# Cutting the first row maximum of each period into 128 and 384 columns, sharing the copy of the value products, and a new order of the period, in an attention and gated-MLP kernel

## The chip, the cores and the metric

The kernel runs on one core of one Trainium2 chip. The metric is the device time of one execution in microseconds (us); lower is better. The profile shown is of one execution, taken by the hardware profiler.

## The reference

```python
# x [1, 2048, 512]; H = 32 heads of Dh = 16
qkv = (x @ wqkv).reshape(B, S, 3, H, Dh).transpose(2, 0, 3, 1, 4)
scores = einsum("bhqd,bhkd->bhqk", q, k) * Dh ** -0.5
o = einsum("bhqk,bhkd->bhqd", softmax(scores), v)
a = o.transpose(0, 2, 1, 3).reshape(B, S, D) @ wo
b = (sigmoid(x @ w_gate) * (x @ w_up)) @ w_down          # F = 1792
g = sigmoid((x * gate_w).sum(-1, keepdims=True))
out = g * a + (1 - g) * b                                # all float32
```

## The kernel before

TensorE (PE) multiplies, ScalarE (ACT) does the exponentials and copies, VectorE (DVE) the row maxima and other copies, GpSimd (POOL) sums, SyncE (SP) issues transfers. Matrices stand as a high and a low part, so that a product of two of them takes three matmuls.

The kernel opens with the projections of the first heads and of the values. Then comes a loop over 256 periods (`for k in range(NPER)`), 16 for each pair of heads; a period deals with two 128-row blocks of keys and half of the queries. Its parts, by the words of the string `STEADY`:

- `m0`, `m1`: the row maxima of a later pair (11 periods ahead), four products of each of the two heads in a period. One takes a score product on PE (L294, 48 rows, 512 columns) into a PSUM tile, and VectorE reduces it to a column of `stat` (L296).
- `t0`, `t1`: four score products of each head (L684), each followed by an exponential on ACT that writes a quarter of a tile `p` (L686). `t1` works one period ahead.
- `d0`, `d1`: six matmuls each (L163) of the sums that fill the rest of PE: projections of later heads and the gate and up products. `d0` uses the lower 64 rows of the PE and `d1` the upper 64, as the two heads do: two products of 64 rows run side by side, one in each half. They write `dn`, which ACT copies out at the end of a period (L609). At `turn` PE waits for a token of POOL, since both halves write one bank.

After these words `values(k)` (L842 to L857) issues eight value products (L848), which the profile counts as 16 matmuls; each writes 17 of the 128 rows of one tile. ACT then copies that tile to `part` or `sum` (L853, 512 columns), and POOL adds `part` to `sum` (L865). From period 245 on (`k >= FREE`) there are no maxima left, another order (`LAST`) holds, and VectorE does that copy (L855). A last part multiplies by `w_down` and `wo`.

The instructions of PE, ACT, DVE and POOL stand in the order in which the code issues them. The layer below writes the semaphore waits. Eight PSUM tiles of one bank each: `dn`, `sm0` to `sm3` (numbers 0 to 3 in the order's words) and `st0` to `st2` (4 to 6). A word such as `m1:3` takes number 3; the value products of each period take number 0 (`SUMS`).

```python
STEADY = ("m1:3 t0:2 m0:4 d1 d1 t0:5 m0:6 d1 d1 t0:1 d1 m0:3 d1 t0:2 turn m0:0 t1:4 "
          "m1:5 d0 d0 t1:1 t1:6 d0 d0 m1:2 d0 m1:3 t1:4 d0")
...
spot[:] = [seven[SUMS]]
values(k)
```

Of the kernel before, what the change touches and what calls it, by code (L numbers as in the profile page):

```python
# [24 lines left out]
S, D, H, DH, F = 2048, 512, 32, 16, 1792  # L25
P = 128
# [20 lines left out]
def gated_mix(ctx, tc, x, xT, wqk, wv, wo, w_gate, w_up, w_down, gate_w, out):  # L47
    nc = tc.nc
    pe, act, dve, pool, sp = nc.tensor, nc.scalar, nc.vector, nc.gpsimd, nc.sync
# [6 lines left out]
    def turns(tiles):  # L56
        turn = iter(range(1 << 30))
        return lambda: tiles[next(turn) % len(tiles)]
# [124 lines left out]
    def work(length):  # L183
# [4 lines left out]
            length -= cost  # L188
        over[0] = max(0.0, -length)

    def flush(queue):
        while queue:
            queue.pop(0)[1]()
# [79 lines left out]
    stat = {}  # L273
# [7 lines left out]
    def sm_step(j):  # L281

        p, s = divmod(j, 32)
        qt, kh = divmod(s, 2)
        qs, ks = QS[p % 2], KS[p % 2]
        half = (p, qt // 8)
        if half not in stat:
            stat[half] = keep.tile([P, 2, 8, 4], F32, name=f"stat{p}_{qt // 8}", tag="stat", bufs=2)
            count[half] = 0

        def one(b, i):
            r, g = 64 * b, 2 * kh + i
            t = bankm()
            pe.matmul(t, qs[r:r + KM, qt * P:(qt + 1) * P], ks[r:r + KM, g * 512:(g + 1) * 512],  # L294
                      start=True, stop=True)
            dve.tensor_reduce(stat[half][:, b, qt % 8, g:g + 1], t, axis=AX.X, op=ALU.max)  # L296
            count[half] += 1
            if count[half] == 64:
                m = mpad()
                dve.tensor_reduce(m[:, :16].rearrange("p (a b) -> p a b", a=2), stat.pop(half), axis=AX.X, op=ALU.max)  # L300
                mt = mrow[half] = keep.tile([P, 32], F32, name=f"mt{p}_{qt // 8}", tag="mt", bufs=2)
                dve.transpose(mt, m)  # L302
        return one

    def put_max(half):
# [309 lines left out]
    def first_max():  # L615
        if first:
            j, i = first.pop(0)
            one = sm_step(j)
            one(0, i)
            one(1, i)  # L620

    for c in range(NC):
        if c + 1 < NC:
# [49 lines left out]
    def st_part(k, b):  # L673

        p, r = divmod(2 * k, 32)
        i, kt = divmod(r, 16)
        qs, ks = QS[p % 2], KS[p % 2]
        r = 64 * b
        pt = ptile[k, b] = mid(f"p{k}_{b}")
        for a in range(2):  # L680
            for c in range(2):
                o = bank()
                q0 = i * 1024 + c * 512
                pe.matmul(o, ks[r:r + KR, (kt + a) * P:(kt + a + 1) * P], qs[r:r + KR, q0:q0 + 512],  # L684
                          start=True, stop=True)
                act.activation(pt[:, 2 * a + c, :], o, AF.Exp, scale=DH ** -0.5)  # L686
                yield

    bank = turns(early)
    ahead = st_part(0, 1)  # L690
# [22 lines left out]
                put_v(t + a, two[a].o, dve if n == 14 or (n == 15 and a == 0) else act)  # L713


    seven = maxb + banks
    bank7 = turns([seven[b] for b in (5, 1, 6, 2, 3, 4, 0)])
    chunks = [(c, f) for c in range(NC) for f in range(0, NF, 2)]

    def hidden_load(c, f):  # L720
# [119 lines left out]
    def values(k):  # L840

        o = bank()  # L842
        half = divmod(k // 8, 2)
        pts = [ptile.pop((k, b)) for b in range(2)]
        for a in range(2):
            for c in reversed(range(4)):
                h = 2 * half[0] + c // 2
                pe.matmul(o[32 * c:32 * c + VW, :], v[:, 2 * k % 16 + a, h * VW:(h + 1) * VW],  # L848
                          pts[c // 2][:, 2 * a + c % 2, :], start=(a == 0), stop=(a == 1))

        def put(e):
            if 2 * k + LEAD < NSTEP:
                act.activation(e, o, AF.Copy)  # L853
            else:
                dve.tensor_copy(e, o)  # L855
        if half not in sums:
            sums[half] = keep.tile([P, 512], F32, name=f"sum{half[0]}_{half[1]}", tag="sum", bufs=2)  # L857
            put(sums[half])
        else:
            e = keep.tile([P, 512], F32, name=f"part{k}", tag="part", bufs=2)  # L860
            put(e)
            later.append((1.3, lambda s=sums[half]: add(s, e)))

        def add(s, e):
            pool.tensor_tensor(s, s, e, ALU.add)  # L865
            if k % 8 == 7:
                sp.dma_start(pv_d[half[1], half[0]], s)

    def mx(b):
        for j in range(LEAD, NSTEP):  # L870
            one = sm_step(j)
            for i in range(2):
                one(b, i)
                yield

    dens = [chain(denominators(0, 0, 32, 8), denominators(1, 0, 32, 8)), denominators(0, 32, 64, 2),
            denominators(1, 32, 64, 2)]
# [5 lines left out]
            yield  # L883

    spot = []

    def emit(order, **parts):

        for word in order.split():
            if word == "turn":  # L890
                if run:
                    turn(run)
                work(2.0)
            else:
                kind, _, b = word.partition(":")
                spot[:] = [seven[int(b)]] if b else []
# [4 lines left out]
    BEGIN = " ".join(w[:-1] + {"1": "5", "5": "1"}.get(w[-1], w[-1]) if ":" in w else w for w in STEADY.split())  # L901
# [4 lines left out]
    bank = bankm = lambda: spot[0]  # L906
    for k in range(NPER):
        n = 2 * k
        if n + LEAD == NSTEP:
            bank = bank7  # L910
            leave = dve.tensor_copy
        if 75 <= k < 123:
            t, r = divmod(k - 75, 6)
            if r in (0, 3):
                split_load(2 * t + r // 3)
            if r in (1, 4):
                split_sum(2 * t + r // 3)
            if r == 1:
                logit_load(2 * t)
            if r in (3, 4):  # L920
                logits(2 * t, r - 3)
        if n % 32 == 0 and n // 32 + 1 < NPAIR:
            load_pair(n // 32 + 1)
        parts["t0"], parts["t1"] = st_part(k, 0), st_part(k + 1, 1) if k + 1 < NPER else iter(())
        emit(BEGIN if k == 0 else STEADY if k < FREE else LAST, **parts)
# [35 lines left out]
    bank = turns(banks[:1])  # L961
    loaded.extend(hidden_load(*chunks[m]) for m in range(2, 4))
    raws.extend(late_raw(*late[m][:2]) for m in range(2, 4))
    loaded.extend(hidden_load(*chunks[m]) for m in range(4, 6))
# [28 lines left out]
        split(oh, ol, ot, act, pool)  # L993
        return oh, ol

    bankt = turns([dn, maxb[1], banks[2], maxb[2], maxb[3]])
    bankh = turns([maxb[0], banks[0], banks[1]])
    acc, had = {}, {}

    def finish(t, o, gate):  # L1000
# [28 lines left out]
    for n, (c, f) in enumerate(chunks):  # L1029
# [5 lines left out]
        for t in range(4):  # L1035
            ops = list(terms([((hl[0][:, a, t * P:(t + 1) * P], hl[1][:, a, t * P:(t + 1) * P]), wd[f + a])
                              for a in range(2)]))
            for m, (a, b) in enumerate(ops):
                pe.matmul(down[t], a, b, start=(f == 0 and m == 0), stop=(f == NF - 2 and m == 5))  # L1039
            if f == NF - 2:  # L1040
                finish(4 * c + t, down[t], g0)
            if (n, t) == (0, 1):
                values(NPER - 1)
                flush(later)
        if n < 3:
            next(dens[1], None)
# [47 lines left out]
```

## Time and profile before

| | |
|---|---|
| median of 3 runs | 1683.34 us (1683.09 to 1683.47) |
| the profiled execution | 1682.99 us, its span 1681.0 us |
| granted PE clock | 1.00 |
| PE busy | 1675.7 us (100%) |
| DVE busy | 1453.0 us (86%) |
| ACT busy | 1360.9 us (81%) |
| POOL busy | 942.5 us (56%) |

The 2.0 us beside the span are start and end of the execution. A busy time is the sum of an engine's own intervals. Matmuls overlap each other in a pipeline and their ends are modelled, so a PE that is always busy need not be one that can do no more.

### The profile page before, as it was taken

What the parts mean: (1) busy time and instruction counts of PE and PEld (TensorE: products, weight loads), DVE (VectorE), ACT (ScalarE), POOL (GpSimd) and SP (SyncE); (2) the same over time, 40 slices, a digit from 0 to 9 for tenths busy, and PEclk for the clock granted to TensorE, in tenths of its full rate; (3) what the DMA queues carried; (4) which work ended last, traced back from release to release, by engine and by line L of the source; (5) the groups of instructions that cost most, each with busy time, mean ns of one, the idle gap of its engine ahead of it and who ended that gap; (6) DMA issues with size and microseconds to landing.
All of it is one profiled execution on the core that took longest, in us unless ns stands there. A gap on an engine that the chain in (4) does not pass through costs nothing.

```text
span 1681.0 us, 34649 instructions
## 1 busy us (share of the span) xinstructions
PE 1675.7 (100%) x12485; PEld 1060.1 (63%) x12485; DVE 1453.0 (86%) x2350; ACT 1360.9 (81%) x2656; POOL 942.5 (56%) x922
## 2 busy tenths in 40 slices
PE   9999999999999999999999999999999999999999
PEld 7766656565656565656565665656565656568887
DVE  7988888888889999999888888889999888887753
ACT  4188888898988898889898989889898989983431
POOL 1134476547656666566666767676666667653110
PEclk9999999999999999999999999999999999999999
DMA  8411447366565564555535353434343434368862
GB/s 271 119 46 59 130 171 211 133 171 206 145 198 136 164 151 154 160 166 188 160 103 146 102 146 108 134 103 133 109 134 105 133 114 158 123 206 277 288 217 70
DMA packets 143788, 254.20 MB, mean 151 GB/s; under 512 B 24256, under 2 KB 36544, under 8 KB 140736
## 3 DMA queue, kind: packets, MB, share of 16 engines
q1 hardware_dynamic: 135024, 235.34, 46.3%
q10 hardware_dynamic: 8592, 16.65, 3.1%
q8 instruction: 98, 1.61, 0.4%
q14 instruction: 74, 0.61, 0.1%
HBM read 149.42 MB, written 102.50 MB: 150 GB/s over the span
## 4 chain that ended last, share of the span: by engine, by line
PE 99%; DVE 0%; DMA 0%; ACT 0%; ACTq 0%; issue 0%; DVEq 0%
PE dn L163 30%; PE sm L848 27%; PE sm L294 16%; PE sm L1039 5%; PE st L684 5%; PE sm L684 5%; PE st L294 2%; PE dn L1039 2%; PE st L1039 2%; PE st L163 2%; PE st L150 1%; PE st L646 1%; PE sm L150 1%; PE st L848 1%; DVE stat L296 0%; DMA x<-in_xT_dram 0%
## 5 line engine op out<-in xcount | busy, mean ns | idle before, releaser
L296 DVE TENSOR_REDUCE stat<-sm 128x1 f32<-128x512 f32 x1314 | 848.2, 681 | 136.6 <-PE sm L684 125.8
L686 ACT ACTIVATE p<-sm 128x512 f32<-128x512 f32 x1030 | 611.0, 630 | 11.3 <-PE st L163 10.1
L686 ACT ACTIVATE p<-st 128x512 f32<-128x512 f32 x1018 | 615.6, 651 | 0.0
L294 PE MATMUL sm<-ks,qs 48*128 48x512 f32 x1314 | 525.2, 435 | 0.0
L848 PE MATMUL sm<-p,v 128*17 128x512 f32 x4016 | 479.9, 595 | 0.0
L296 DVE TENSOR_REDUCE stat<-st 128x1 f32<-128x512 f32 x734 | 478.8, 680 | 0.0
L684 PE MATMUL sm<-qs,ks 64*128 64x512 f32 x1030 | 428.6, 419 | 0.0
L684 PE MATMUL st<-qs,ks 64*128 64x512 f32 x1018 | 425.5, 419 | 0.0
L294 PEld LDWEIGHTS sm<-ks,qs 48*128 48x128 f32 x1314 | 241.0, 184 | 261.7 <-DVE stat L296 214.9
L865 POOL TENSOR_TENSOR sum<-sum,part 128x512 f32<-128x512 f32 x224 | 288.6, 1288 | 135.5 <-PE sm L684 121.7
L294 PE MATMUL st<-ks,qs 48*128 48x512 f32 x734 | 290.0, 395 | 0.0
L848 PEld LDWEIGHTS sm<-p,v 128*17 128x17 f32 x4016 | 93.1, 96 | 224.3 <-issue 155.4
L853 ACT ACTIVATE part<-sm 128x512 f32<-128x512 f32 x214 | 128.3, 600 | 124.1 <-issue 84.1
L544 POOL TENSOR_TENSOR chain<-chain,chain 128x512 f32<-128x512 f32 x96 | 124.3, 1294 | 155.4 <-PE sm L684 140.4
L684 PEld LDWEIGHTS st<-qs,ks 64*128 64x128 f32 x1018 | 187.3, 184 | 29.6 <-issue 3.4
L684 PEld LDWEIGHTS sm<-qs,ks 64*128 64x128 f32 x1030 | 190.0, 185 | 10.5 <-issue 5.1
L544 POOL TENSOR_TENSOR had<-chain,had 128x512 f32<-128x512 f32 x96 | 123.6, 1287 | 39.4 <-PE sm L684 17.8
L294 PEld LDWEIGHTS st<-ks,qs 48*128 48x128 f32 x734 | 137.0, 187 | 1.5 <-ACT v L667 0.5
L609 ACT ACTIVATE chain<-dn 128x512 f32<-128x512 f32 x128 | 88.2, 689 | 0.0
L544 POOL TENSOR_TENSOR side<-side,side 128x512 f32<-128x512 f32 x32 | 41.4, 1294 | 77.9 <-PE sm L684 71.9
L105 POOL TENSOR_TENSOR ol<-ot,oh 128x512 fp32r<-128x512 f32 (+1 forms) x8 | 14.7, 1842 | 102.7 <-ACT oh L102 81.5
L321 POOL CAST mhl<-mt 128x32 fp32r<-128x32 f32 x32 | 7.6, 238 | 101.0 <-DVE mt L302 101.0
(912 smaller groups left out, 3251.5 us busy)
## 6 DMA issues: line engine op xcount, KB each, us to landing
gul<-gu_d SPq DMA_DIRECT2D x56, 512.0 KB
had<-gu_d SPq DMA_DIRECT2D x84, 256.0 KB
gu_d<-had SPq DMA_DIRECT2D x84, 256.0 KB
gu_d<-side SPq DMA_DIRECT2D x56, 256.0 KB
pv_d<-sum SPq DMA_DIRECT2D x32, 256.0 KB
qs<-q_d SPq DMA_DIRECT2D x30, 256.0 KB
ks<-k_d SPq DMA_DIRECT2D x30, 256.0 KB
gu_d<-far SPq DMA_DIRECT2D x28, 256.0 KB
```

The lines of the kernel that those rows point to most:

```text
L150: pe.matmul(o, a, b, start=(i == 0), stop=(i == len(ops) - 1))
L163: mm = pe.matmul(self.o, a[rows], b[rows], start=(self.n == 0), stop=(self.n == 2 * len(self.ops) - 1))
L294: pe.matmul(t, qs[r:r + KM, qt * P:(qt + 1) * P], ks[r:r + KM, g * 512:(g + 1) * 512], start=True, stop=True)
L296: dve.tensor_reduce(stat[half][:, b, qt % 8, g:g + 1], t, axis=AX.X, op=ALU.max)
L544: pool.tensor_tensor(to, u, w, ALU.add)
L609: leave = lambda e, o: act.activation(e, o, AF.Copy)
L684: pe.matmul(o, ks[r:r + KR, (kt + a) * P:(kt + a + 1) * P], qs[r:r + KR, q0:q0 + 512], start=True, stop=True)
L686: act.activation(pt[:, 2 * a + c, :], o, AF.Exp, scale=DH ** -0.5)
L848: pe.matmul(o[32 * c:32 * c + VW, :], v[:, 2 * k % 16 + a, h * VW:(h + 1) * VW], pts[c // 2][:, 2 * a + c % 2, :], start=(a == 0), stop=(a ...
L853: act.activation(e, o, AF.Copy)
L865: pool.tensor_tensor(s, s, e, ALU.add)
L1039: pe.matmul(down[t], a, b, start=(f == 0 and m == 0), stop=(f == NF - 2 and m == 5))
```

## The change

1. The first product of `m0` in each period, which is now the first product behind the value products, is cut: 128 columns, then one `t1` product, then the other 384 columns, into the same PSUM tile (`CUT`). Each part has its own reduction, and `stat` has five columns instead of four; where the same columns of the other head aren't cut, one reduction gives two values.
2. The copy of the value products is shared (`SHARE`): ACT copies 384 columns, VectorE 128. It stays whole on ACT in the periods that `busy` names, in which VectorE has other work. The instructions of the copy are issued at the start of the next period.
3. The order of the period is written anew. `m0:1=-11` now means: slot 1, in the tile that slot 11 of the period before had; `t0:8=1`: slot 8, in that of this period's slot 1. So a word's tile changes from period to period. The value products take the tile of slot 9, the fifth maximum (`m1:9`). The special order of the first period is gone. A tile `p` is taken when a part is set up, not at its first step.

POOL's instructions stand in the same order as before; SP issues 1062 transfers in both, some of them in another sequence.

```diff
+CUT = 128
+SHARE = 384
...
+        def scores(t, b, g, cols):
+            r = 64 * b
+            pe.matmul(t[:, cols], qs[r:r + KM, qt * P:(qt + 1) * P],
+                      ks[r:r + KM, g * 512 + cols.start:g * 512 + cols.stop], start=True, stop=True)
+
+        def one(b, i, cut=False):
+            g = 2 * kh + i
             t = bankm()
+            to = stat[half][:, b, qt % 8]
+            if cut:
+                for a, cols in enumerate((slice(0, CUT), slice(CUT, 512))):
+                    if a:
+                        yield
+                    scores(t, b, g, cols)
+                    dve.tensor_reduce(to[:, a:a + 1], t[:, cols], axis=AX.X, op=ALU.max)
+            else:
+                scores(t, b, g, slice(0, 512))
+                if g:
+                    dve.tensor_reduce(to[:, g + 1:g + 2], t, axis=AX.X, op=ALU.max)
+                else:
+                    dve.tensor_reduce(to[:, :2], t.rearrange("p (a c) -> p a c", a=2), axis=AX.X, op=ALU.max)
...
         def put(e):
-            if 2 * k + LEAD < NSTEP:
-                act.activation(e, o, AF.Copy)
+            if k >= FREE:
+                dve.tensor_copy(e, o)
+                return
+            n = 512 if busy(k) else SHARE
+            act.activation(e[:, :n], o[:, :n], AF.Copy)
+            if n < 512:
+                dve.tensor_copy(e[:, n:], o[:, n:])
...
+    def busy(k):
+        return (78 <= k + 1 < 123 and (k + 1 - 75) % 6 in (3, 4)) or (192 <= k < 215 and k % 8 != 4) or k >= NPER - 13
...
     def mx(b):
...
-                one(b, i)
-                yield
+                yield from one(b, i, cut=b == 0 and j % 2 == 0 and i == 0)
...
-    STEADY = ("m1:3 t0:2 m0:4 d1 d1 t0:5 m0:6 d1 d1 t0:1 d1 m0:3 d1 t0:2 turn m0:0 t1:4 "
-              "m1:5 d0 d0 t1:1 t1:6 d0 d0 m1:2 d0 m1:3 t1:4 d0")
-    SUMS = 0
+    STEADY = ("m0:1=-11 t1:2=-12 m0 t0:3=-15 d1 d1 m0:4=-16 d1 d1 t0:5=-13 d1 m0:6=-14 m0:7=-17 t0:8=1 d1 m1:9=2 "
+              "t0:10=3 t1:11=4 turn d0 m1:12=5 d0 m1:13=6 d0 m1:14=8 d0 d0 t1:15=7 d0 t1:16=10")
...
     for k in range(NPER):
         n = 2 * k
+        while leaving:
+            leaving.pop()()
...
-        spot[:] = [seven[SUMS]]
-        values(k)
+        if k < FREE:
+            spot[:] = [slots["9"]]
+            before, slots = {**slots, "17": spot[0]}, {}
+        leaving.append(values(k))
+        if k >= FREE:
+            leaving.pop()()
```

In the built program, PE's row before, from the end of the value products of period 74 on (`p74_0` is a tile `p`, `v` the values, `ks1`, `qs1` keys and queries of the maxima's pair, `dn_68` the sums of `d1`; the brackets name the engine or queue whose semaphore a row waits for):

```order
L848 MATMUL sm0_69<-p74_0_6031,v_99 17x512 x2
L294 MATMUL sm3_72<-ks1_103,qs1_102 128x512 [waits DVE_49]
L684 MATMUL sm2_71<-qs0_100,ks0_101 128x512
L294 MATMUL st0_65<-ks1_103,qs1_102 128x512 [waits Activation_49]
L163 MATMUL dn_68<-xh_107,side(0, 0)h_5410 128x512 [waits DMAHW3_49,Activation_49]
L163 MATMUL dn_68<-xl_108,side(0, 0)h_5410 128x512 [waits DMAHW4_49]
```

and PE's row now, at the same place:

```order
L872 MATMUL sm1_70<-p74_0_6251,v_99 17x512 x2
L299 MATMUL st2_67<-ks1_103,qs1_102 128x128 [waits Activation_49]
L709 MATMUL st0_65<-qs0_100,ks0_101 128x512 [waits DVE_49]
L299 MATMUL st2_67<-ks1_103,qs1_102 128x384 [waits DVE_49]
L709 MATMUL sm3_72<-qs0_100,ks0_101 128x512 [waits Activation_49]
L165 MATMUL dn_68<-xh_107,side(0, 0)h_5604 128x512 [waits DMAHW3_49,Activation_49]
L165 MATMUL dn_68<-xl_108,side(0, 0)h_5604 128x512 [waits DMAHW4_49]
```

The maximum's product became two, with a `t1` product between them, and the second waits for VectorE: the count that it asks for is the one that the reduction of the first part brings. All 245 second parts wait like this.

VectorE's row before, behind those same value products (`sm3` is `m1:3`, the first maximum):

```order
L296 TENSOR_REDUCE stat5_0_5698<-sm3_72 128x1 [waits PE_49] x2
L296 TENSOR_REDUCE stat5_0_5698<-st0_65 128x1 [waits PE_49]
L296 TENSOR_REDUCE stat5_0_5698<-st2_67 128x1 [waits PE_49]
L296 TENSOR_REDUCE stat5_0_5698<-sm3_72 128x1 [waits PE_49]
L296 TENSOR_REDUCE stat5_0_5698<-sm0_69 128x1 [waits PE_49]
```

VectorE's row now (the copy's tile `part74`, then the two parts of the cut maximum, both from `st2`), up to the fifth maximum (`st0`, with two values):

```order
L882 COPY part74_6314<-sm1_70 128x128 [waits Activation_49]
L312 TENSOR_REDUCE stat5_0_5907<-st2_67 128x1 [waits PE_49] x2
L316 TENSOR_REDUCE stat5_0_5907<-st1_66 128x1 [waits PE_49]
L316 TENSOR_REDUCE stat5_0_5907<-sm2_71 128x1 [waits PE_49]
L316 TENSOR_REDUCE stat5_0_5907<-sm1_70 128x1 [waits PE_49]
L318 TENSOR_REDUCE stat5_0_5907<-st0_65 128x2 [waits PE_49]
```

The new copy stands ahead of the reductions and waits for ACT: the count is that of ACT's copy of the other 384 columns. There are 207 such copies, and 38 periods in which ACT copies all 512 columns.

ACT's row now, at the same place:

```order
L632 ACTIVATE side00_10_6303<-dn_68 128x512
L880 ACTIVATE part74_6314<-sm1_70 128x384 [waits DVE_49,PE_49,Pool_49]
L711 ACTIVATE p76_1_6320<-st0_65 128x512 [waits PE_49,Activation_49]
L711 ACTIVATE p75_0_6319<-sm3_72 128x512 [waits PE_49]
L711 ACTIVATE p75_0_6319<-sm0_69 128x512 [waits PE_49]
```

The copy keeps its place ahead of the period's exponentials; the first exponential is now one of `t1`.

More of the change, by code (lines that the diff above doesn't have):

```diff
@@ L189, in work, with flush_steps @@
         over[0] = max(0.0, -length)
+    def flush_steps(steps):
+        for _ in steps:
+            pass
     def flush(queue):
@@ L287, in sm_step @@
         if half not in stat:
-            stat[half] = keep.tile([P, 2, 8, 4], F32, name=f"stat{p}_{qt // 8}", tag="stat", bufs=2)
+            stat[half] = keep.tile([P, 2, 8, 5], F32, name=f"stat{p}_{qt // 8}", tag="stat", bufs=2)
             count[half] = 0
-        def one(b, i):
-            r, g = 64 * b, 2 * kh + i
-            t = bankm()
-            pe.matmul(t, qs[r:r + KM, qt * P:(qt + 1) * P], ks[r:r + KM, g * 512:(g + 1) * 512],
-                      start=True, stop=True)
-            dve.tensor_reduce(stat[half][:, b, qt % 8, g:g + 1], t, axis=AX.X, op=ALU.max)
+        def scores(t, b, g, cols):
[4 more added lines that the diff above has]
+            g = 2 * kh + i
+            t = bankm()
+            to = stat[half][:, b, qt % 8]
[11 more added lines that the diff above has]
+                    dve.tensor_reduce(to[:, :2], t.rearrange("p (a c) -> p a c", a=2), axis=AX.X, op=ALU.max)
             count[half] += 1
@@ L618, in first_max @@
             one = sm_step(j)
-            one(0, i)
-            one(1, i)
+            for b in range(2):
+                flush_steps(one(b, i))
     for c in range(NC):
@@ L679, in st_part, with steps @@
         pt = ptile[k, b] = mid(f"p{k}_{b}")
[L680 to L686, printed above, removed]
-                yield
+        def steps():
+            for a in range(2):
+                for c in range(2):
+                    o = bank()
+                    q0 = i * 1024 + c * 512
+                    pe.matmul(o, ks[r:r + KR, (kt + a) * P:(kt + a + 1) * P], qs[r:r + KR, q0:q0 + 512],
+                              start=True, stop=True)
+                    act.activation(pt[:, 2 * a + c, :], o, AF.Exp, scale=DH ** -0.5)
+                    yield
+        return steps()
     bank = turns(early)
@@ L851, in put, with leave_sums @@
         def put(e):
-            if 2 * k + LEAD < NSTEP:
-                act.activation(e, o, AF.Copy)
-            else:
[L855 to L862, printed above, removed]
+            if k >= FREE:
[5 more added lines that the diff above has]
+                dve.tensor_copy(e[:, n:], o[:, n:])
+        def leave_sums():
+            if half not in sums:
+                sums[half] = keep.tile([P, 512], F32, name=f"sum{half[0]}_{half[1]}", tag="sum", bufs=2)
+                put(sums[half])
+            else:
+                e = keep.tile([P, 512], F32, name=f"part{k}", tag="part", bufs=2)
+                put(e)
+                later.append((1.3, lambda s=sums[half]: add(s, e)))
         def add(s, e):
@@ L894, in emit @@
             else:
[L895 to L896 removed]
+                kind, _, slot = word.partition(":")
+                if slot:
+                    slot, _, of = slot.partition("=")
+                    old, of = of[0] == "-", of.strip("-")
+                    spot[:] = [(before if old else slots)[of]]
+                    slots[slot] = spot[0]
                 next(parts[kind], None)
[L899 to L902 removed]
+    STEADY = ("m0:1=-11 t1:2=-12 m0 t0:3=-15 d1 d1 m0:4=-16 d1 d1 t0:5=-13 d1 m0:6=-14 m0:7=-17 t0:8=1 d1 m1:9=2 "
+              "t0:10=3 t1:11=4 turn d0 m1:12=5 d0 m1:13=6 d0 m1:14=8 d0 d0 t1:15=7 d0 t1:16=10")
+    seven = maxb + banks
+    before = dict(zip(("11", "12", "15", "16", "13", "14", "17"), (seven[b] for b in (3, 2, 4, 1, 6, 5, 0))))
     LAST = "t0 d1 t0 d1 t0 d1 turn t0 t1 t1 d0 t1 d0 t1 d0"
@@ L906, in gated_mix @@
     bank = bankm = lambda: spot[0]
+    leaving = []
     for k in range(NPER):
         n = 2 * k
+        while leaving:
+            leaving.pop()()
         if n + LEAD == NSTEP:
-            bank = bank7
+            last = [before[s] for s in ("11", "12", "15", "16", "13", "14", "17")]
+            bank = turns(last)
             leave = dve.tensor_copy
@@ L924, in gated_mix @@
         parts["t0"], parts["t1"] = st_part(k, 0), st_part(k + 1, 1) if k + 1 < NPER else iter(())
-        emit(BEGIN if k == 0 else STEADY if k < FREE else LAST, **parts)
+        emit(STEADY if k < FREE else LAST, **parts)
         if run and run.done():
@@ L960, in gated_mix @@
         pass
-    bank = turns(banks[:1])
+    tail = dict(zip((5, 1, 6, 2, 3, 4, 0), last))
+    bank = turns([tail[4]])
     loaded.extend(hidden_load(*chunks[m]) for m in range(2, 4))
@@ L1042, in gated_mix @@
             if (n, t) == (0, 1):
-                values(NPER - 1)
+                values(NPER - 1)()
                 flush(later)
```

10 lines of the change are left out of this document (5 added, 5 removed).

## Prediction

> **What bounds the kernel now.** I read the page's busy times first, then its chain, then the waits, and last the timeline of one period, since a period is repeated 245 times.
>
> ```profile
> span 1681.0 us, 34649 instructions
> PE 1675.7 (100%) x12485; PEld 1060.1 (63%) x12485; DVE 1453.0 (86%) x2350; ACT 1360.9 (81%) x2656; POOL 942.5 (56%) x922
> ...
> PE 99%; DVE 0%; DMA 0%; ACT 0%; ACTq 0%; issue 0%; DVEq 0%
> ...
> PEld sm L294 <- DVE stat L296: 214.9, 278, 0.9
> ...
> DVE stat L296 <- PE sm L684: 125.8, 187, 0.9
> ...
> PEld sm L848 <- DVE stat L296: 66.0, 244, 0.4
> ```
>
> PE looks full, and the chain stays on it. But the last row says that the weight load of the value products waited for a reduction 244 times, once in nearly every period, so PE and VectorE hold each other. One period, by the timeline of PE and then of VectorE:
>
> ```profile
> 619.30 1.91 PE L848 MATMUL sm<-p,v 128*17 128x512 f32 x16
> 621.14 0.50 PE L294 MATMUL sm<-ks,qs 48*128 48x512 f32 x1
> ...
> 621.48 0.39 PE L163 MATMUL dn<-xh,side(0, 3)h 64*128 64x512 f32 x1
> ...
> 621.71 0.39 PE L163 MATMUL dn<-xl,side(0, 3)h 64*128 64x512 f32 x1
> ...
> 623.02 0.50 PE L684 MATMUL st<-qs,ks 64*128 64x512 f32 x1
> ...
> 624.87 0.62 PE L848 MATMUL sm<-p,v 128*17 128x512 f32 x4
> ```
>
> ```profile
> 619.70 1.28 DVE L296 TENSOR_REDUCE stat<-sm 128x1 f32<-128x512 f32 x2
> ...
> 621.67 0.69 DVE L296 TENSOR_REDUCE stat<-sm 128x1 f32<-128x512 f32 x1
> 622.28 0.68 DVE L296 TENSOR_REDUCE stat<-st 128x1 f32<-128x512 f32 x1
> ...
> 623.48 1.28 DVE L296 TENSOR_REDUCE stat<-sm 128x1 f32<-128x512 f32 x2
> ```
>
> I count from the start of the value products, 619.30. The next product starts at 1.84, its reduction at 2.37. Five reductions follow each other at 0.60 (two take 1.28, one 0.68); the fifth is the second of the pair at 623.48 and ends at 624.76, 5.46. It frees tile 0, and 0.11 later, at 5.57, the next value products start. So the period of 5.57 is 1.84 + 0.53 + 4 x 0.60 + 0.68 + 0.11, give or take 0.01. Behind the fifth, three more reductions run beside the value products, and VectorE then idles until the first new product.
>
> **The parts of the change.** *The new order, without its waits.* Five maxima still stand between one block of value products and the next, now the cut one and four whole ones (the fifth is `m1:9`, whose tile the value products take). So the cycle has the same links, and what changes is when the first reduction can run. Each other move is priced at nothing, covered by slack that remains: `stat` has 16 more elements once in 16 periods; the first exponential being `t1` swaps equals on ACT; SP's resequenced transfers are no releasers in the rows above; POOL keeps its order, and the later issue of the copy leaves its place in ACT's row. If that cover were gone, the largest of them would be a late `t1` exponential, some 0.1 a period.
>
> *The shared copy* (207 periods). Its rows:
>
> ```profile
> 621.32 0.60 ACT L853 ACTIVATE part<-sm 128x512 f32<-128x512 f32 x1 [0.57 <-issue]
> ...
> L102 ACT ACTIVATE hl<-gul 128x1024 fp32r<-128x1024 f32 x26 | 27.4, 1052 | 13.6 <-DVE gul L766 10.5 <-PE sm L1039 3.1
> ...
> L102 ACT ACTIVATE xh<-x 128x512 fp32r<-128x512 f32 x15 | 8.3, 624 | 1.6 <-DMA x<-in_xT_dram 1.6
> ...
> 16.52 0.60 ACT L228 ACTIVATE qe<-st 128x512 fp32r<-128x512 f32 x1 [2.01 <-PE st L646]
> ...
> 17.16 0.69 DVE L229 TENSOR_TENSOR qe<-st,qe 128x512 fp32r<-128x512 f32 x1 [1.24 <-ACT qe L228]
> ...
> 604.28 0.22 DVE L300 TENSOR_REDUCE mpad<-stat 128x16 f32<-128x64 f32 x1
> ...
> 1452.60 0.39 DVE L778 TENSOR_SCALAR gul<-gul 128x512 f32<-128x512 f32 x1
> ```
>
> ACT's copy starts 2.02 behind the value products. From 512 to 1024 columns ACT's copies grow by 0.43, so 128 columns less are 0.11 less: 0.49 (ends: 0.45, strictly by columns, and 0.60, nothing saved). In the order, VectorE's copy waits for that copy to end; from ACT's end at 17.12 to VectorE's start at 17.16 it took 0.04. So VectorE's copy starts at 2.02 + 0.49 + 0.04 = 2.55. Its length for 128 columns is not in the trace: between 0.22 (a reduction of 64) and 0.39 (the cheapest 512 columns); on the line from 0.22 at 64 to 0.68 at 512 it is 0.29, which I take. The next operation follows 0.08 before its end (0.60 against 0.68), so at 2.76. Queued behind this waiting copy are all reductions of the period, and behind them PE. What ACT saves, 0.11, is of no use: its row shows 0.57 of idle time ahead of the copy already.
>
> *The cut.* The first part's reduction is the operation at 2.76 and ends 0.29 later, at 3.05 (its product was there long before: 1.84 + 0.53 less 384 columns, 0.17 at the 0.23 a 512-column product takes in one half of the PE, from 621.48 to 621.71; that is 2.20). The second part's product waits for that reduction. A held product starts 0.06 after the release: the reduction at 622.28 ends at 622.96 and the `t1` product that it holds starts at 623.02. So 3.11. From such a start to the reduction it is 0.53 less 0.06 for 128 columns: 0.47, hence 3.58. Behind the held product stands everything else that PE has to do in the period, since its row is in order.
>
> *From there to the next value products.* The second part's reduction takes the engine for 0.55 - 0.08 = 0.47 (384 columns on the same line), then three at 0.60, 0.68 to the end of the fifth, 0.11 to the value products: 3.06. PE adds a little: from 3.11 it needs 0.50 - 0.39 = 0.11 for weights that weren't loaded ahead and 0.17 for 384 columns, then by the order four pairs at 0.23 until `m0:6`, at 4.31; its reduction can begin 0.42 later, 4.73, and VectorE would be free at 3.58 + 0.47 + 0.60 = 4.65. So 0.08 more. The period is 3.58 + 3.06 + 0.08 = 6.72, against 5.57: 1.15 longer.
>
> *The 38 periods without sharing.* The first part's reduction starts at 2.20, ends at 2.49; held product 2.55; second reduction 3.02; 3.02 + 3.06 + 0.08 = 6.16: 0.59 longer. In 16 of them a product for the gate stands on VectorE ahead; it may add 0.1 there, 2 us in all, which I leave to the range.
>
> Counts come from rows of the trace and the order:
>
> ```profile
> L853 ACT ACTIVATE part<-sm 128x512 f32<-128x512 f32 x214 | 128.3, 600 | 124.1 <-issue 84.1 <-PE sm L848 9.6 <-POOL mh L358 2.9
> ...
> L853 ACT ACTIVATE sum<-sm 128x512 f32<-128x512 f32 x31 | 18.6, 599 | 17.1 <-PE sm L848 17.1
> ```
>
> These are 245 periods; 207 share. The sum: 207 x 1.15 = 238, 38 x 0.59 = 22, together 260. The profiled execution took 1682.99, its span of 1681.0 and 2.0 around it; 1681 + 260 + 2 = 1943, and that execution is 0.35 below the median, so 1944 against 1683.34. The ends: with 0.22 for both small VectorE operations, 0.45 for ACT's copy and no PE term, a shared period is 1.15 - 0.14 - 0.04 - 0.08 = 0.89 longer and an unshared one 0.44, 201 us, 1884. With 0.39 twice, 0.60 on ACT, 0.06 for every release being 0.11, and 0.08 for the reduction that gives two values, it is 1.15 + 0.20 + 0.11 + 0.05 + 0.08 = 1.59 and about 0.82: 360 us, 2043.
>
> *A rule weighed.* In the trace of before no bank is read by two engines at a time, or read while PE writes it: ACT reads tile 0 from 621.32 on, and PE writes it again at 624.87, after VectorE's reduction of it has ended at 624.76. The Trainium skill, PSUM — Partial Sum Buffer, section "PSUM bank collisions raise a hardware error", states that two engines must not touch the same bank in the same 32 partitions at once, disjoint columns and two reads included, and asks for semaphores by bank, not by address. By that rule both waits of the order are needed and the sum is 1944; if columns apart were enough, it would be that of the first rival, 1674. The trace agrees in so far as it shows no such overlap; none of its rows tests one.
>
> **The rivals.** *First, on the other side: neither wait costs.* If VectorE's copy started when the value products end and the second part weren't held:
>
> ```profile
> 1454.26 1.91 PE L848 MATMUL sm<-p,v 128*17 128x512 f32 x16
> ...
> 1456.34 0.69 DVE L855 COPY part<-sm 128x512 f32<-128x512 f32 x1 [3.35 <-PE sm L848]
> ```
>
> The copy would start at 2.08, the first part at 2.29, the second at 2.50; 2.50 + 3.06 = 5.56. With 2.20 and 2.41 (but not before its product, about 2.50) in the other periods it is the same: 0.01 to 0.04 less than now, up to 10 us, 1674. It decides when the second reduction starts by 5.57 - 3.06 = 2.51; I have it at 3.58. For it speaks VectorE's idle time, against it both waits in the order. Chance 4%.
>
> *Second: only the held product costs*, because VectorE is still at old reductions when ACT's copy ends. Then every period is 0.59 longer, 245 x 0.59 = 145, 1828. It needs VectorE busy until 2.55; the pair at 619.70 ends at 1.68, so against it stands 0.87 of idle time. 6%. *Third: only the copy's wait costs*, the held product not: the second part at 2.97, 6.03 with no PE term, 207 x 0.46 = 95, 1778. 3%.
>
> *Fourth: PE pays more after the break.* Its products behind the held one are then in a row of late releases; if three more in a period found their weights not loaded ahead (0.11 each), it is 1.48 and 0.92: 341 us, 2025. For it: the 0.50 at 623.02 is such a case now. Against it: tiles and exponentials have slack in the longer period. 10%.
>
> **How the numbers follow.** The forecast, both waits at full cost, has 77%: 1944. From 1890 to 2015 reaches over most of its own ends and a part of the fourth. A difference of 0.2% (3.4 us) is about what can be told from no change. Faster: the first rival, 4%. The same: 1%, where its gain comes to nothing. Slower: 95%.
>
> **What would show it.** Right: value products 6.7 apart in most periods and 6.1 to 6.2 around 192 to 215; the 384-column weight load waiting for VectorE some 245 times, and VectorE's copy for ACT 207 times; PE idle for about a microsecond in each period; ACT's copy near 0.49 and VectorE's small operations near 0.29. Wrong: if the 384-column product starts within 0.4 of the 128-column one, the hold is not there; if value products keep 5.6, the first rival holds; if VectorE's copy starts right behind its last reduction, it is the second.

## The result and the profile after

The changed kernel takes 1939.15 us (median of 4 runs, 1938.05 to 1941.95) against 1683.40 of the kernel before, run beside it: a ratio of 1.1519, 95% interval 1.1499 to 1.1539. It was forecast slower at 1944, and slower it is. The profiled execution took 1938.05, its span 1936.3.

The page of the kernel after, its span, its busy times and its chain, and the three rows of its waits that are new (us in total, times, the longest):

```profile
span 1936.3 us, 35227 instructions
PE 1764.6 (91%) x12730; PEld 1095.0 (57%) x12730; DVE 1538.5 (79%) x2802; ACT 1434.9 (74%) x2656; POOL 940.2 (49%) x922
...
PE 66%; DVE 11%; ACT 9%; issue 6%; POOL 5%; DMA 2%; SPq 0%; POOLq 0%; ACTq 0%; DVEq 0%
...
DVE part L882 <- ACT part L880: 149.4, 181, 2.7
PEld sm L299 <- DVE stat L312: 139.0, 140, 1.3
PEld st L299 <- DVE stat L312: 104.7, 105, 2.8
```

PE was busy for 100% of the span and is for 91%; its chain share fell from 99% to 66%. No engine is full any more. VectorE's copy waited for ACT 181 times into `part` (another 26 copies go into `sum`, together 207), and the weight load of the 384-column product waited for the reduction on L312 140 + 105 = 245 times, once for each cut product. One period by the timelines of PE, then VectorE, then ACT:

```profile
661.96 1.91 PE L872 MATMUL st<-p,v 128*17 128x512 f32 x16
663.80 0.32 PE L299 MATMUL sm<-ks,qs 48*128 48x128 f32 x1
663.81 0.50 PE L709 MATMUL sm<-qs,ks 64*128 64x512 f32 x1
665.06 0.44 PE L299 MATMUL sm<-ks,qs 48*128 48x384 f32 x1 [0.75 <-DVE stat L312]
...
665.34 0.40 PE L709 MATMUL st<-qs,ks 64*128 64x512 f32 x1
...
666.05 0.39 PE L299 MATMUL st<-ks,qs 48*128 48x512 f32 x1
```

```profile
664.51 0.29 DVE L882 COPY part<-st 128x128 f32<-128x128 f32 x1 [0.89 <-ACT part L880]
664.72 0.28 DVE L312 TENSOR_REDUCE stat<-sm 128x1 f32<-128x128 f32 x1
665.54 0.56 DVE L312 TENSOR_REDUCE stat<-sm 128x1 f32<-128x384 f32 x1 [0.53 <-PE sm L299]
666.01 0.69 DVE L316 TENSOR_REDUCE stat<-sm 128x1 f32<-128x512 f32 x1
666.62 1.28 DVE L316 TENSOR_REDUCE stat<-st 128x1 f32<-128x512 f32 x2
667.82 0.68 DVE L318 TENSOR_REDUCE stat<-sm 128x2 f32<-128x512 f32 x1
```

```profile
663.99 0.49 ACT L880 ACTIVATE part<-st 128x384 f32<-128x384 f32 x1 [0.54 <-POOL side_9r L473]
```

Count from the value products at 661.96. ACT's copy starts at 2.03 and takes 0.49; VectorE's copy starts at 2.55; the first part's reduction at 2.76; the held product at 3.10, after PE did nothing for 0.75; its reduction at 3.58. Four whole ones follow; the last, the fifth maximum, ends at 6.54, and the next value products start at 6.67. The value products of this kind of period are 6.67 apart in the median, and 6.11 to 6.18 in most of those where ACT copies all 512 columns, against 5.57 before.

### The profile page after: what moved, and what is told of

The parts are those of the page before. It is cut to its first block, busy times and chain, and to the rows that moved or that the text cites. A ratio compares the mean times of both kernels' runs of the same rounds, so it can differ in the third digit from the quotient of the medians.

```text
span 1936.3 us, 35227 instructions
## 1 busy us (share of the span) xinstructions
PE 1764.6 (91%) x12730; PEld 1095.0 (57%) x12730; DVE 1538.5 (79%) x2802; ACT 1434.9 (74%) x2656; POOL 940.2 (49%) x922
## 4 chain that ended last, share of the span: by engine, by line
PE 66%; DVE 11%; ACT 9%; issue 6%; POOL 5%; DMA 2%; SPq 0%; POOLq 0%; ACTq 0%; DVEq 0%
PE dn L165 14%; PE sm L299 9%; PE sm L709 7%; PE sm L872 7%; PE st L299 6%; PE st L709 5%; PE st L872 5%; ACT part L880 5%; DVE stat L316 4%; DVE stat L312 3%; PE st L1086 3%; PE sm L1086 3%; DVE part L882 3%; PE dn L1086 2%; ACT chain L632 2%
## 5 line engine op out<-in xcount | busy, mean ns | idle before, releaser
L316 DVE TENSOR_REDUCE stat<-sm 128x1 f32<-128x512 f32 x906 | 590.9, 683 | 0.2
L299 PE MATMUL sm<-ks,qs 48*128 48x512 f32 (+1 forms) x1348 | 493.1, 405 | 95.0 <-DVE stat L312 85.0
L711 ACT ACTIVATE p<-st 128x512 f32<-128x512 f32 x876 | 516.4, 606 | 77.8 <-PE st L709 68.8
L299 PE MATMUL st<-ks,qs 48*128 48x512 f32 (+1 forms) x945 | 358.0, 405 | 71.8 <-DVE stat L312 67.3
L709 PE MATMUL st<-qs,ks 64*128 64x512 f32 x876 | 349.2, 423 | 0.0
L872 PE MATMUL sm<-p,v 128*17 128x512 f32 x2336 | 279.1, 595 | 0.0
L872 PE MATMUL st<-p,v 128*17 128x512 f32 x1760 | 210.4, 595 | 0.0
L312 DVE TENSOR_REDUCE stat<-sm 128x1 f32<-128x128 f32 (+1 forms) x280 | 117.6, 420 | 76.6 <-PE sm L299 76.1
L312 DVE TENSOR_REDUCE stat<-st 128x1 f32<-128x128 f32 x210 | 88.2, 420 | 57.2 <-PE st L299 56.7
L318 DVE TENSOR_REDUCE stat<-sm 128x2 f32<-128x512 f32 x162 | 109.5, 681 | 0.0
```

Source lines behind the costliest of these rows:

```text
L299: pe.matmul(t[:, cols], qs[r:r + KM, qt * P:(qt + 1) * P], ks[r:r + KM, g * 512 + cols.start:g * 512 + cols.stop], start=True, stop=True)
L312: dve.tensor_reduce(to[:, a:a + 1], t[:, cols], axis=AX.X, op=ALU.max)
L316: dve.tensor_reduce(to[:, g + 1:g + 2], t, axis=AX.X, op=ALU.max)
L318: dve.tensor_reduce(to[:, :2], t.rearrange("p (a c) -> p a c", a=2), axis=AX.X, op=ALU.max)
```

## The experiments

The first three take the change apart. The next ones ask whether the cut or the sharing could pay without its wait. The last ones follow a loss that the first three brought to light. Periods and pauses are read from the profiled execution of each run.

**One part at a time.** Without the sharing (ACT copies all 512 columns in every period):

```diff
-SHARE = 384
+SHARE = 512
```

> ACT copies all 512 columns in every period (no VectorE copy, so no copy that waits for ACT); the cut product in one PSUM tile and the new order stay. Theory, both waits cost and add up: every period is then like the changed kernel's unshared ones, 6.13 us between value products (around 192 to 215), 0.56 more than the 5.57 of before; 245 x 0.56 = 137, so about 1820 us. Rival, the new order of the period costs and not the waits: it stays near 1939. Rival, only the held product costs: the copy was free, so 1939 as well.

Measured: 1828.8 us, ratio 1.0862 (1.0847 to 1.0877), the period 6.125 in the median. Without the cut, but with the sharing:

```diff
-                yield from one(b, i, cut=b == 0 and j % 2 == 0 and i == 0)
+                yield from one(b, i)
...
-    STEADY = ("m0:1=-11 t1:2=-12 m0 t0:3=-15 ...
+    STEADY = ("m0:1=-11 t1:2=-12 t0:3=-15 ...
```

> The first maximum's product is whole again (one product, one reduction); the copy stays shared in 207 periods, and the new order stays. Theory: VectorE's copy still starts 2.55 behind the value products and the first reduction 0.21 later at 2.76 instead of 2.37; four more at 0.60, 0.68 to the end, 0.11 to the next value products: 5.95 in the 207 periods, 5.57 in the others; 207 x 0.38 = 79, about 1762 us. Rival, the order costs: near 1939. Rival, only the held product costs: 1683.

Measured: 1769.7 us, 1.0515 (1.0499 to 1.0532), the period 5.947. With both edits at once only the new order is left, and what came with it (the fifth column of `stat`, the later issue of the copy):

> Neither cut nor shared copy: the new order and the tiles that change from period to period alone. Theory, only the two waits cost: five whole maxima still stand between value products, first reduction at 2.37, period 5.57, 1683 us within 8. Rival, the order is what costs: between 1750 and 1939. Rival, the order gains by itself (first product no longer held by the eighth reduction of the period before): up to 0.1 a period, 1660.

Measured: 1696.89 us, 1.0083 (1.007 to 1.0097), a miss by some 14 us, though the median period is 5.577 as before. The two times above, each some 8 us over its expectation, hold this loss too. VectorE in one period of the kernel without sharing (its value products start at 629.77), and then in one of the kernel without the cut (630.01):

```profile
631.97 0.29 DVE L312 TENSOR_REDUCE stat<-st 128x1 f32<-128x128 f32 x1 [0.53 <-PE st L299]
632.79 0.56 DVE L312 TENSOR_REDUCE stat<-st 128x1 f32<-128x384 f32 x1 [0.53 <-PE st L299]
```

```profile
632.57 0.29 DVE L882 COPY part<-sm 128x128 f32<-128x128 f32 x1 [0.87 <-ACT part L880]
632.77 0.68 DVE L318 TENSOR_REDUCE stat<-sm 128x2 f32<-128x512 f32 x1
```

Cut alone: the first reduction starts at 2.20, the second only at 3.02, with 0.53 of VectorE idle between, for 384 columns that the hold kept back. Shared alone: the period's first reduction starts at 2.76, behind a copy that VectorE spent 0.87 waiting for. So each wait costs by itself: the hold 1828.8 - 1696.9 = 132 us (245 periods, 0.54 each), the copy 1769.7 - 1696.9 = 73 us (207 periods, 0.35 each). Together they cost more than their sum, 1939.2 - 1696.9 = 242 against 205. The rows say why for most of it: the copy moves the first reduction to 2.76 in either case, but from 2.20 with the cut and from 2.37 (as before) without it; 0.17 more in 207 periods are 35 us.

**The cut without its hold.** The second part gets a PSUM tile of its own, and ACT copies all 512 columns:

```diff
                     if a:
                         yield
+                        t = bankm()
...
-    STEADY = ("m0:1=-11 t1:2=-12 m0 t0:3=-15 d1 d1 m0:4=-16 d1 d1 t0:5=-13 d1 m0:6=-14 m0:7=-17 t0:8=1 d1 m1:9=2 "
+    STEADY = ("m0:1=-11 t1:2=-13 m0:18=-12 t0:3=-15 d1 d1 m0:4=-16 d1 d1 t0:5=-14 d1 m0:6=-17 m0:7=1 t0:8=18 d1 m1:9=2 "
```

> The cut stays 128 and 384, but the second part goes into a PSUM tile of its own (the one that slot 12 of the period before had; the slots behind take one tile later each), so that it need not wait for the reduction of the first; ACT copies all 512 columns. It has the same number of matmuls and of reductions as with the whole copy and the cut in one tile. Theory, the hold is what the cut costs: first reduction at 2.20, second at 2.40 to 2.50, then 3.06: 5.46 to 5.56, so 1656 to 1681 us. Rival, the additional product and reduction cost by themselves: about 1820, as with the hold.

Measured: 1695.75 us, 1.0076 (1.0063 to 1.0089). The hold is gone, and with it 133 us against the kernel that only cuts; so the 245 additional products and reductions don't explain the loss. But the cut doesn't gain either: the time is above the 1656 to 1681 expected, and the median period is 5.575, as before. VectorE, in the period that starts at 1292.12, and two products of PE beside it:

```profile
1294.32 0.79 DVE L313 TENSOR_REDUCE stat<-st 128x1 f32<-128x128 f32 x2 [0.53 <-PE st L299]
1295.02 0.68 DVE L317 TENSOR_REDUCE stat<-sm 128x1 f32<-128x512 f32 x1
1295.70 1.29 DVE L317 TENSOR_REDUCE stat<-st 128x1 f32<-128x512 f32 x2
```

```profile
1295.05 0.39 PE L299 MATMUL st<-ks,qs 48*128 48x512 f32 x1
...
1295.23 0.40 PE L165 MATMUL dn<-xl,cb(0, 5)h 64*128 64x512 f32 x1
```

The first reduction starts 0.17 earlier than in the kernel before, at 2.20, but two parts take 0.70 of the engine (1294.32 to 1295.02) where one whole took 0.60. And `m0:6`, whose product ended at 1295.44, is reduced only from 1295.70, while VectorE was free at about 1295.62 (0.60 behind 1295.02). Ahead of `m0:6` in PE's row stands the fifth `d1` matmul; it runs in the other half of the PE and ends at 1295.63. The reduction seems to have gone by that: over 220 periods of this trace it starts 0.07 or more behind this end, never ahead of it. So the next edit puts this `d1` behind `m0:6`:

```diff
-    ... t0:5=-14 d1 m0:6=-17 m0:7=1 t0:8=18 d1 m1:9=2 "
+    ... t0:5=-14 m0:6=-17 d1 m0:7=1 t0:8=18 d1 m1:9=2 "
```

> The cut in two tiles, whole copy on ACT, and one matmul of d1, the fifth, moved from ahead of m0:6 to behind it. In the run with two tiles the reduction of m0:6 began at 3.58 although its product had ended at 3.32 and VectorE was free at 3.50; the matmul ahead of it in PE's row, the fifth of d1, ended at 3.5. Theory, PE's count reaches a product only when all ahead of it in the row have ended: m0:6 then starts at 3.50, the period is 5.48, 245 x 0.09 = 22, and the isolated pauses of about 12 us in sum stay: about 1673 us. Rival, the reduction was late for another reason (VectorE): 1696, no change.

Measured: 1689.44 us, 1.0031 (1.0021 to 1.0042), the period 5.551. VectorE, from value products at 1292.99 on, and the value products that follow:

```profile
1295.19 0.79 DVE L313 TENSOR_REDUCE stat<-sm 128x1 f32<-128x128 f32 x2 [0.58 <-PE sm L299]
1295.89 1.89 DVE L317 TENSOR_REDUCE stat<-sm 128x1 f32<-128x512 f32 x3
1297.70 0.68 DVE L319 TENSOR_REDUCE stat<-st 128x2 f32<-128x512 f32 x1
```

```profile
1298.20 0.39 PE L165 MATMUL dn<-xh,ca(1, 5)l 64*128 64x512 f32 x1
1298.54 1.91 PE L873 MATMUL st<-p,v 128*17 128x512 f32 x16
```

VectorE's row is closed now: no gap from the first reduction to the fifth, which ends at 1298.38. The value products come 0.16 later, not 0.11: PE's last `d0` matmul ahead of them starts only at 1298.20, and with 0.23 for it and 0.11 for weights loaded late (both taken from other rows), PE is there at 1298.54. By this sum PE's own row sets the end now. Of the 0.09 a period that was expected 0.02 came, and the time missed the 1673 expected. The limits of VectorE and PE lie within some 0.1 us of each other.

**The sharing without its wait.** Two tiles for the cut, and VectorE copies its 128 columns first, ACT its 384 behind it:

```diff
             n = 512 if busy(k) else SHARE
-            act.activation(e[:, :n], o[:, :n], AF.Copy)
             if n < 512:
                 dve.tensor_copy(e[:, n:], o[:, n:])
+            act.activation(e[:, :n], o[:, :n], AF.Copy)
```

> The cut in two tiles as before it, and the copy shared again in 207 periods, but VectorE copies its 128 columns first and ACT's 384 wait for it. Theory, what sharing cost was VectorE's place behind ACT: VectorE copies from 2.08 to 2.37, first reduction 2.29, second 2.50, third whole one at 3.57 as without sharing; ACT starts at 2.41 instead of 2.02 and has about 0.5 idle ahead of its copy. So 5.57 to 5.62 a period: 1696 to 1708 us, against 1695.75 without sharing. Rival, two engines on one bank cost what they cost whoever goes first: 0.38 in 207 periods, about 1775 us.

Measured: 1735.38 us, 1.0305 (1.0291 to 1.032), the period 5.79 where it shares: between the two expectations. The value products stand at 1348.60 and 1354.39; VectorE, then ACT, then PE at the period's end, and one of its waits:

```profile
1350.65 0.29 DVE L882 COPY part<-st 128x128 f32<-128x128 f32 x1 [0.57 <-PE st L873]
1350.85 0.28 DVE L313 TENSOR_REDUCE stat<-sm 128x1 f32<-128x128 f32 x1
1351.05 0.55 DVE L313 TENSOR_REDUCE stat<-st 128x1 f32<-128x384 f32 x1
...
1353.37 0.68 DVE L319 TENSOR_REDUCE stat<-sm 128x2 f32<-128x512 f32 x1
```

```profile
1350.97 0.49 ACT L883 ACTIVATE part<-st 128x384 f32<-128x384 f32 x1 [0.90 <-DVE part L882]
1351.36 0.59 ACT L712 ACTIVATE p<-sm 128x512 f32<-128x512 f32 x1
```

```profile
1354.05 0.41 PE L710 MATMUL st<-qs,ks 64*128 64x512 f32 x1
1354.39 1.05 PE L873 MATMUL sm<-p,v 128*17 128x512 f32 x8
```

```profile
PEld sm L710 <- ACT p L712: 42.5, 140, 0.3
```

VectorE is not late: its fifth maximum ends at 1354.05, 5.45 behind the value products. But ACT's copy starts at 2.37 instead of 2.03, all exponentials stand behind it, and the last product of PE's row (the `t1` score at 1354.05) takes a tile that an exponential has to give back: such weight loads waited for ACT 210 times (140 into `sm`, 70 into `st`), against 11 times without sharing. The wait changed engines and went on through ACT; part of ACT's idle time was no slack.

**Where the order alone loses 14 us.** Its span is 14.4 longer than before: 10.5 in the 256 periods (8.9 of it from 48 to 63 and from 112 to 143), 3.7 in what follows the periods, 0.2 ahead. For the pauses, first a wait of the new order alone, from 805 to 815; then PE, the first product behind each of two pauses; then the first of them in a table by windows (length; busy times of PE, its weight loads, VectorE, ACT and POOL; granted clock, DMA share, GB/s):

```profile
ACT part L880 <- DMA qs<-q_d: 3.8, 1, 3.8
```

```profile
372.29 0.50 PE L299 MATMUL st<-ks,qs 48*128 48x512 f32 x1 [1.02 <-ACT part L880]
...
807.91 0.79 PE L299 MATMUL st<-ks,qs 48*128 48x512 f32 x1 [2.39 <-ACT part L880]
```

```profile
372.00:373.00 1.00, 0.71 (x4) 0.48 (x4) 0.22 (x2) 1.00 (x3) 0.00 (x0) 1.00 1.04 383
373.00:374.00 1.00, 1.00 (x7) 0.54 (x7) 1.00 (x2) 1.00 (x3) 0.70 (x1) 0.85 1.03 365
374.00:375.00 1.00, 1.00 (x7) 0.81 (x8) 0.53 (x2) 1.00 (x3) 0.58 (x1) 0.50 0.90 305
...
377.00:378.00 1.00, 1.00 (x16) 0.27 (x8) 0.00 (x0) 0.48 (x1) 0.00 (x0) 0.94 0.89 281
```

In the second pause an issue of ACT's own transfers (`mixed_x`) stands ahead of its copy and waits for a transfer of SP's, the next pair's queries; the copy comes 3.8 late, and PE stops for 2.39. It doesn't need those queries: in the trace the two transfers report their landing on one and the same semaphore, and the issue stands until the earlier one, issued at 799.74, has landed at 806.75. In the kernel before the same issue has another semaphore and doesn't wait. The first pause is of this kind too, with another transfer of SP's. Behind both the granted clock is 0.50 for some microseconds. I tried to take the meeting away, first by giving the 28 transfers of `mixed_x` to SP:

```diff
-            act.dma_start(xs[:, k0:k0 + 2, cols].bitcast(F32), ...
+            sp.dma_start(xs[:, k0:k0 + 2, cols].bitcast(F32), ...
```

> Neither cut nor sharing (the new order alone), and the 28 transfers that bring mixed tokens back are issued by SP instead of ACT. The order alone took 1696.9 although its period is 5.57; it paused at two places, 2.9 and 5.5 us, where ACT's issue of such a transfer stood in the queue ahead of the copy and waited for a transfer of SP. Theory, these pauses are what the order costs: 1683 to 1686 us. Rival, the pauses come with the transfers whoever issues them, or SP's queue is held instead: 1695 or more.

Measured: 1695.84 us, 1.0066 (1.0052 to 1.0079), as the rival had it. The long pause only moved, to period 128 (10.82); in it POOL, and behind POOL the PE, wait for a weight transfer in SP's queue:

```profile
POOL chain_0r L473 <- DMA chain_7r<-in_w_up_dram: 5.3, 1, 5.3
```

The same edit in the kernel with two tiles and the later `d1`:

> Both: the cut in two tiles, whole copy, the fifth matmul of d1 behind m0:6, and the 28 transfers on SP. Theory: the gains add, 1683 - 22 = about 1661 us (1658 to 1668), faster than before. Rival, pauses remain: 1673.

Measured: 1688.04 us, 1.0025 (1.0016 to 1.0033), above both expectations: periods of 8.50 at 128 and 7.47 at 238 remain, and the others are of 5.55. Then the call that loads the next pair was moved two periods down in the code, once with two tiles and the later `d1`, once with the order alone:

```diff
-        if n % 32 == 0 and n // 32 + 1 < NPAIR:
+        if n % 32 == 4 and n // 32 + 1 < NPAIR:
```

> The order with two PSUM tiles for the cut and the later fifth sum, and the next pair's queries and keys loaded two periods later. Theory: the long pause at period 127 is the meeting of that load with ACT's own transfer issue, and goes when they no longer meet: some 7 us less than 1689.4, about 1682. Rival: ACT's issue then meets another transfer of SP, the pause moves, and the time stays at 1687 to 1691.

Measured: 1690.85 us, 1.0044 (1.003 to 1.0058), as the rival had it; periods of 9.95 at 127 and 7.38 at 238 are left.

> The new order alone (no cut, no sharing), and the next pair's queries and keys loaded two periods later. Theory: the pauses at periods 127 and 128, 5.5 us together, go, and the one at period 50 (2.9 us), which has another transfer behind it, stays: about 1691 against 1696.9 of the order alone. Rival: the pauses move, 1695 to 1698.

Measured: 1698.03 us, 1.0093 (1.0079 to 1.0107), close to the rival; in the profiled execution, the slowest of its four, 8.18 at 50 and 10.48 at 127 are left and 8.21 at 67 is new. In none of the four kernels did the pauses go. With `mixed_x` on SP, the long one met a weight transfer instead. With the later call it met the same transfer as ever, here by the order alone:

```profile
ACT part L880 <- DMA qs<-q_d: 4.1, 1, 4.1
```

SP issued the first transfer of that load in period 126 all the same (at 794.6 and 803.6, against 799.7 in the order alone): the edit didn't make it later, so these two runs don't test the meeting. What stays open is which move in the sequence of transfers gives ACT's issue that semaphore.

The 3.7 us behind the periods are no pause. The products there by one pair of tensors, in the kernel before and in the changed one (count, busy time in us, mean ns of one):

```profile
L1039 PE MATMUL dn<-wd_h,hl 128*128 128x512 f32 x64 | 22.3, 389 | 0.0
L1086 PE MATMUL dn<-wd_h,hl 128*128 128x512 f32 x64 | 22.7, 395 | 0.0
```

Some 800 products follow each other there, at 0.2267 us before and 0.231 in the changed kernel, with the granted clock at 1.00 until the last microseconds; 0.0046 each make 3.7. Every kernel with the new order has this loss, 3.7 to 4.0; the tile `dn` is the same in both, so the PSUM tile doesn't explain it. What makes these products slower was not tested.

No version beats the kernel before. 1688.04 is the nearest, and in its profiled execution the periods take no longer than before: it loses 3.7 behind them and 1.1 ahead of them.

## Why the prediction was right

*The held product.* Forecast at 3.11 and its reduction at 3.58; the rows show 3.10 and 3.58. That the hold alone costs 132 us and vanishes with a second tile shows the cause: not the number of products, but that both parts lie in one tile. The 132 us are 0.54 for a cut product, against 0.59 forecast.

*The shared copy.* ACT's copy at 2.02 and 0.49 long, VectorE's at 2.55, its length 0.29, the reduction at 2.76: 2.03, 0.49, 2.55, 0.29 and 2.76 were measured. The line between a reduction of 64 and one of 512 columns gave the right length for 128, for the copy and for the reduction.

*From there to the next value products* stood 3.06 and a PE term of 0.08. The period came out at 6.67, not 6.72, so this is the term that was mis-sized. The product of `m0:6` started at 666.05, which is 4.09, not 4.31. The 0.28 for late weights and 384 columns was right: the next product of that half starts 0.28 behind the held one. But from there to `m0:6` it takes three steps of 0.23 to 0.24, not the four that were counted. So it was ready before VectorE was free for it at 666.62, and the PE term of 0.08 was nothing. VectorE's row alone sets the rest, 3.09 in place of 3.06.

*The unshared periods*: 6.16 was forecast, 6.13 measured in the median. Four of the 16 with the gate's product take 6.37 to 6.58, which is within the 2 us left for them. *The reduction that gives two values*, for which 0.08 was held ready in the range, costs nothing. One line of the trace of after, by source:

```profile
L318 DVE TENSOR_REDUCE stat<-sm x162: 650/681/683, 29.2 to 1701.2; 128x2 f32<-128x512 f32 x162
```

Its median of 681 ns stands against 0.68 for one value.

*The sum.* 260 was forecast for the periods. They are 250.6 longer: 207 of 1.10 and 38 of 0.56 make 249, and a pause of 1.9 in period 127 the rest, within 0.3. But the span grew by 255.3, since 1.0 came ahead of the periods, where the first cut lies, and 3.7 behind them. *The new order at nothing* was the term that was wrong: by itself it costs 14 us, 8.9 of them in two stretches with pauses, where ACT's issue waits for a transfer of SP's, which had been called no releasers, and 3.7 in slower products behind the periods. In the changed kernel less of this shows: the 3.7, and the 1.9 in period 127, where ACT idles for 2.3 ahead of its copy, at its own issues. That its longer period leaves the transfers more time is a guess that no run tests. The total is partly luck: the periods were forecast 9 us too long, and nearly 5 us outside them were not forecast at all.

*The rivals.* That neither wait costs is refuted by the three kernels that take the change apart. Only the held product at 1828 and only the copy at 1778 come near the kernels that have one wait each, 1828.8 and 1769.7, in part by luck: the waits were 132 and 73, not the 145 and 95 of these sums, and the order's 14 filled all or most of the gap. For this kernel they fail: VectorE is idle when ACT's copy ends, so both act. More weights loaded late would have shown as a longer stretch between 3.58 and the end, and that came out shorter. The rule weighed there (the Trainium skill, PSUM — Partial Sum Buffer, section "PSUM bank collisions raise a hardware error": keep engines apart by bank, not by address) is what the program's waits follow, in both places; the trace agrees in that the hold went when the second part got a tile in another bank. Every tile here is a whole bank, so no run tells a wait by bank from a wait by tile, and none lets two engines meet in one bank.

## What to carry to other kernels

Cutting a product so that its reduction can begin earlier gains nothing inside one PSUM tile: the second part waits for the first one's reader, here 0.54 us in each of 245 periods. A share of a copy given to an engine stands in that engine's row, and if it waits there, everything behind it waits as well; price it by when its partner ends, not by its length. In a cycle that three engines close within 0.1 us, 0.1 or 0.2 us freed on one of them is worth next to nothing, and a new order has to be read for its transfers, too, down to the semaphores that they share.

## What was not expected of the hardware

The granted clock fell to 0.50 around short pauses of PE. In the order alone, after a pause of 1.02 us that ended at 372.29, it was 0.50 from 373.71 to 377.12, for 3.41 us; in the pause of 2.39 us it fell at 807.20, 1.7 us after PE's last matmul had ended, and stayed at 0.50 until 814.02, for 6.83 us. But the length of a pause doesn't decide it. The changed kernel has pauses of about 0.75 us in most periods and one of 2.5 us in period 127, and its clock was at 1.00 all the while, as a window of each shows (PE busy for 0.31 and for 0.00 of 1.00, clock 1.00):

```profile
664.00:665.00 1.00, 0.31 (x2) 0.00 (x0) 0.48 (x2) 1.00 (x2) 0.91 (x2) 1.00 0.00 0
933.00:934.00 1.00, 0.00 (x0) 0.00 (x0) 0.00 (x0) 0.08 (x1) 0.00 (x0) 1.00 0.94 227
```

A pause of 1.7 us in period 238 of the kernel with two tiles, the later `d1` and `mixed_x` on SP left the clock at 1.00 too, while one of 1.0 us at 371 in the order alone with the later load was followed by 3.41 us at 0.50. The times of the changes in the order alone lie on a grid: from 373.71 to 807.20 it is 433.49 us, which is 127 times 3.413. So it may matter where in this grid a pause falls; that alone doesn't sort the pauses of these runs, and what does stays open.

So a kernel with 9% of idle PE kept its full clock, while two rare pauses of another did not. At half the clock for 10.24 us, PE lost up to 5.1 us of its full speed, in stretches that cost 8.9 us; how much of the one is in the other isn't separated. The Trainium skill, TensorE: Matmul & The Clock Gate, section "Part 1: The HAM clock gate", has the clock halved after an idle window of about 3.4 us; here 1.02 us were enough, while the lengths of the slow stretches, 3.41 and 6.83 us, agree with one and two such windows.

The other finding is of the two halves of PE: a reader of a product in one half was released only when the matmul of the other half that stood ahead in PE's row had ended (1295.63, not 1295.44), which left VectorE idle for 0.08 us in a period until that matmul was moved behind. The ends are modelled; the move is what speaks for it, for with it the idle time went.
